# Attention and MLP on one core: the first MLP layer of the last two token chunks as seven products of quarters

## The chip, the cores and the metric

The kernel runs on one NeuronCore of a Trainium2 chip. The metric is the device time of one execution in microseconds (us), the median of three runs. The engines are called TensorE (PE in a profile; PEld is its weight load), VectorE (DVE), ScalarE (ACT), GpSimd (POOL) and SyncE (SP). SBUF is the on-chip working memory of 128 partitions, PSUM the memory in eight banks per partition into which TensorE writes its products.

## The reference

Attention with a threshold, and on its result a two-layer MLP with a squared ReLU, all in fp32.

```python
# q, k, v: (8 batches, 8 heads, 576 rows, 64); tau = 0.02
scores = q @ k.T / sqrt(64)
thresh = max(scores, axis=-1) - tau
scores = where(scores >= thresh, scores, -1e9)
attn   = softmax(scores)
x      = (attn @ v) as (8*576 = 4608 tokens, 8*64 = 512)

# w_in: (512, 2048), w_out: (2048, 512)
h   = x @ w_in
g   = maximum(h, 0) ** 2
out = g @ w_out                      # (4608, 512)
```

## The kernel before

The 4608 tokens are 18 chunks of 256. Attention runs in steps, and TensorE's matmuls of the MLP are put between the steps in small pieces. A chunk's pieces are queued when the attention output of its tokens is complete. With the last mix of attention weights and values, the chunks 15, 16 and 17 become complete together, and after it only the MLP of these three is left.

`fill` takes the pieces in order. What a piece leaves to other engines (`then`) is recorded after the next piece, so that TensorE's next matmuls stand ahead of it.

```python
P, TCH = 128, 256                  # tokens of a block and of a chunk
NMC, NFT, HF, HD = 4, 16, 8, 256   # d_model/128, d_ff/128, half of NFT, half of d_model
w_in_sb = const.tile([P, NMC, d_ff], FP32)
wo      = const.tile([P, 7, HF, HD], FP32)      # w_out in four quarters, and three sums of quarters
xT      = const.tile([P, NMC, 5 * TCH], FP32)   # attention output, a ring of five chunks
g       = const.tile([P, NFT, TCH], FP32)
gsum    = [const.tile([P, HF, P], FP32) for i in range(2)]
...
    def square_half(lo):
        f = slice(lo, lo + HF // 2)
        nc.gpsimd.tensor_tensor(out=gsum[0][:, f, :], in0=g[:, f, P:], in1=g[:, lo + HF:lo + HF + HF // 2, P:], op=ALU.add)
        nc.gpsimd.tensor_tensor(out=gsum[1][:, f, :], in0=gsum[0][:, f, :], in1=g[:, f, 0:P], op=ALU.subtract)

    def mlp_in(j, x):                           # first layer of chunk j, 128 of the 2048 columns
        f, at = FORDER[x], j * TCH % RING
        if x % 2 == 0:
            used["h"] = take("mm", (6, 7)) if j < PLAIN else next_bank()
        h = used["h"].rearrange("p (f n) -> p f n", f=2)
        for c in range(NMC):
            nc.tensor.matmul(h[:, x % 2, :], w_in_sb[:, c, f * P:(f + 1) * P], xT[:, c, at:at + TCH],
                             start=(c == 0), stop=(c == NMC - 1))
        ...
        if x % 2:
            def square():
                to = g[:, f - 1:f + 1, :]
                nc.scalar.activation(out=to, in_=h, func=AF.Relu)
                nc.gpsimd.tensor_tensor(out=to, in0=to, in1=to, op=ALU.mult)
                if j >= PLAIN and x % 8 == 7:
                    square_half(x // 8 * (HF // 2))
            posts.append(square)
        return posts
```

The second layer of all chunks but the first already works by seven products of quarters (in Strassen's manner, in Winograd's form): a chunk's g and w_out are each cut into four quarters, and seven products of quarters, or of sums of quarters, take the place of eight.

```python
    PRODUCTS = ("1", "5", "6", "2", "7", "4", "3")

    def product(j, x, half):
        if half == 0:
            used["p"] = next_bank()
        to = used["p"][:, 0:HD]
        p = PRODUCTS[x]
        ...
        g0, g1 = g[:, 0:HF, :], g[:, HF:, :]
        left, slot = {"1": (g0[:, :, 0:P], Q00), "5": (gsum[0], FT1), "6": (gsum[1], FT2), "2": (g1[:, :, 0:P], Q10),
                      "7": (gsum[0], FT3), "4": (g1[:, :, P:], FT4), "3": (gsum[1], Q11)}[p]
        for f in range(half * HF // 2, (half + 1) * HF // 2):
            nc.tensor.matmul(to, left[:, f, :], wo[:, slot, f, :], start=(f == 0), stop=(f == HF - 1))
        if not half:
            return []
        ...
        def then():
            add, sub, tt, u = ALU.add, ALU.subtract, nc.vector.tensor_tensor, u_sum
            if p == "1":
                nc.scalar.copy(p1s, to)
            elif p == "5":
                nc.scalar.copy(p5s, to)
                halves(lambda f: tt(out=gsum[0][:, f, :], in0=g0[:, f, 0:P], in1=g0[:, f, P:], op=sub))
            elif p == "6":
                tt(out=u, in0=to, in1=p1s, op=add)
                nc.gpsimd.tensor_tensor(out=osb[:, 0, HD:], in0=p5s, in1=u, op=add)
                halves(lambda f: tt(out=gsum[1][:, f, :], in0=g1[:, f, 0:P], in1=gsum[1][:, f, :], op=sub))
            ...
            else:                               # product 3, the last
                tt(out=osb[:, 0, HD:], in0=to, in1=osb[:, 0, HD:], op=add)
                return [lambda: store_rows(j, 0, 1)]
        return [then]

    def pieces_of(j):
        todo = [((x // 4 + 1) * NMC, mlp_in, j, x) for x in range(NFT)]
        if j < PLAIN:                           # PLAIN = 1: chunk 0 alone
            todo += [...]
        else:
            todo += [(n_pieces, product, j, x, half) for x in range(len(PRODUCTS)) for half in range(2)]
        return todo
```

Of the kernel before, what the change touches and what calls it, by code (L numbers as in the profile page):

```python
# [9 lines left out]
FP32 = mybir.dt.float32  # L10
U32 = mybir.dt.uint32
AF = mybir.ActivationFunctionType
ALU = mybir.AluOpType
# [6 lines left out]
def kernel(  # L20
# [10 lines left out]
    nc = tc.nc  # L31
    B, H, S, D = q.shape
    d_model, d_ff = moe_w_in.shape
    n_tokens = out.shape[0]
    P = 128
# [6 lines left out]
    NFT = d_ff // P  # L42
    TCH = 2 * P
    NCH = n_tokens // TCH
    HF, HD = NFT // 2, d_model // 2
# [6 lines left out]
    psum = ctx.enter_context(tc.tile_pool(name="psum", bufs=1, space=bass.MemoryType.PSUM))  # L52
# [4 lines left out]
    w_in_sb = const.tile([P, NMC, d_ff], FP32, name="w_in_sb")  # L57
# [7 lines left out]
    WP = 512  # L65
# [6 lines left out]
    wT = const.tile([P, NC9, S + REST], FP32, name="wT")  # L72
# [3 lines left out]
    at = RAW * 2 * WP  # L76
    w_slots = [const.tile([P, 2, S], FP32, name=f"w{i}") for i in range(2)]
# [6 lines left out]
    qT = const.tile([P, S], FP32, name="qT")  # L84
    kT = [const.tile([P, S], FP32, name=f"kT{i}") for i in range(2)]
    RING = 5 * TCH
    xT = const.tile([P, NMC, RING], FP32, name="xT")
    KB = S // 32
    NB = 2 * KB * 2 * 32
    turned = const.tile([P, 2 * NB], FP32, name="turned")  # L90
    assert 3 * 3 * WP <= 2 * NB
    g = const.tile([P, NFT, TCH], FP32, name="g")
    gsum = [const.tile([P, HF, P], FP32, name=f"gsum{i}") for i in range(2)]
# [8 lines left out]
    bank = {}  # L102
# [3 lines left out]
    n_pieces = n_in + NFT * d_model // WP  # L106
# [202 lines left out]
    used = {"tx": 0, "mm": 0, "bank": 7}  # L309

    def take(what, among):
        used[what] += 1
        return bank[among[used[what] % len(among)]]

    def next_bank():

        among = (4, 5, 6, 7) if state["step"] > first_dma + 2 else (6, 7)
        used["bank"] = min([x for x in among if x > used["bank"]] or among)
        return bank[used["bank"]]
# [144 lines left out]

    def square_half(lo):

        f = slice(lo, lo + HF // 2)
        nc.gpsimd.tensor_tensor(out=gsum[0][:, f, :], in0=g[:, f, P:], in1=g[:, lo + HF:lo + HF + HF // 2, P:], op=ALU.add)  # L470
        nc.gpsimd.tensor_tensor(out=gsum[1][:, f, :], in0=gsum[0][:, f, :], in1=g[:, f, 0:P], op=ALU.subtract)

    def mlp_in(j, x):
# [8 lines that stand above are left out]
        if x == NFT - 1:  # L482
            read_to["x"] = (j + 1) * TCH
        posts = []
        if j == PLAIN:
            posts.append(lambda: some_sums(1))
        if x % 2:
# [8 lines that stand above are left out]
# [4 lines left out]
    def some_sums(count):  # L500


        done = 16 - len(sums)
        count = min(count, (16 if state["free"] else 6 if state["rounded"] == n_pieces else 0) - done)
        for to, a, b, part in sums[:count]:
            f = slice(part * 2, part * 2 + 2)
            nc.vector.tensor_tensor(out=wo[:, to, f, :], in0=wo[:, a, f, :], in1=wo[:, b, f, :], op=ALU.subtract)  # L507
        del sums[:count]
# [21 lines left out]
    def store_rows(j, t0, t1):  # L530
        lo = j * TCH
        nc.gpsimd.dma_start(out=out[lo + t0 * P:lo + t1 * P, :].rearrange("(t p) d -> p t d", p=P), in_=osb[:, t0:t1, :])
# [5 lines left out]
    def product(j, x, half):  # L538

        if half == 0:  # L540
            used["p"] = next_bank()
        to = used["p"][:, 0:HD]
        p = PRODUCTS[x]
        if sums:
            need = {"5": 4, "6": 8, "4": 12, "7": 16}.get(p, 0)
            some_sums(max(need - 16 + len(sums), 1))
            assert state["free"]
        g0, g1 = g[:, 0:HF, :], g[:, HF:, :]
        left, slot = {"1": (g0[:, :, 0:P], Q00), "5": (gsum[0], FT1), "6": (gsum[1], FT2), "2": (g1[:, :, 0:P], Q10),
                      "7": (gsum[0], FT3), "4": (g1[:, :, P:], FT4), "3": (gsum[1], Q11)}[p]  # L550
        for f in range(half * HF // 2, (half + 1) * HF // 2):
            nc.tensor.matmul(to, left[:, f, :], wo[:, slot, f, :], start=(f == 0), stop=(f == HF - 1))  # L552
        if not half:
            return []

        def halves(fn):
            for lo in (0, HF // 2):
                fn(slice(lo, lo + HF // 2))
# [12 lines that stand above are left out]
            elif p == "2":  # L571
                tt(out=osb[:, 0, 0:HD], in0=to, in1=p1s, op=add)
            elif p == "7":
                tt(out=u, in0=to, in1=u, op=add)
                nc.gpsimd.tensor_tensor(out=osb[:, 1, HD:], in0=p5s, in1=u, op=add)
            elif p == "4":
                tt(out=osb[:, 1, 0:HD], in0=u, in1=to, op=sub)
                return [lambda: store_rows(j, 1, 2)]
            else:
                tt(out=osb[:, 0, HD:], in0=to, in1=osb[:, 0, HD:], op=add)  # L580
                return [lambda: store_rows(j, 0, 1)]
        return [then]


# [5 lines left out]
    def paired(n):  # L590

        return n >= 3 * HP
# [6 lines left out]
    PLAIN = 1  # L599

    def by_dma(n):

        return n >= 3 * HP - 1
# [6 lines left out]
    for s, (n, i) in enumerate(steps):  # L610
# [5 lines left out]
        if i in mixed:  # L616
            first, lag = mixed[i]
            cols = slice(first * P, S if by_dma(n) else min((i + 1) * P, S))
# [6 lines left out]
    chunk_at, j = {}, 0  # L625
# [12 lines left out]
    def pieces_of(j):  # L638

        todo = [((x // 4 + 1) * NMC, mlp_in, j, x) for x in range(NFT)]  # L640
        if j < PLAIN:
            todo += [(n_in + min(f + 1 + f // (NFT - 2), NFT), mlp_out, j, f) for f in range(NFT)]
        else:
            todo += [(n_pieces, product, j, x, half) for x in range(len(PRODUCTS)) for half in range(2)]
        return todo

    def add_chunk(j):
        waiting.extend(pieces_of(j))
# [17 lines left out]
    def after():  # L666
        now = state["last"]
        state["last"] = []
        for fn in state["then"]:
            state["last"] += fn() or []  # L670
        state["then"] = []
        for fn in now:
            fn()

    def fill(us):
        state["left"] += us
        while waiting and state["left"] >= PIECE_US / 2 and waiting[0][0] <= state["usable"]:
            _, fn, *what = waiting.popleft()
            state["left"] -= PIECE_US
            if fn is mlp_out or what[0] <= PLAIN and what[1] == 0:  # L680
                after()
            then = fn(*what)
            after()
            state["then"] = then
        state["left"] = min(state["left"], PIECE_US)
# [3 lines left out]
    for s, (n, i) in enumerate(steps):  # L689
        if s < HP * FIRST:  # L690
            x = int(n > 0 and i == 0)
        else:
            x = 2 if (n, i) in ((2 * HP - 2, FIRST + 1), (2 * HP - 1, FIRST + 1), (2 * HP, FIRST)) else 1
# [14 lines left out]
    for s, (n, i) in enumerate(steps):  # L708
# [20 lines left out]
        if more:  # L729
            a, b, c, d = (s + 1, s + 5, s + 7, s + 8) if paired(n) else (s + 1, s + 2, s + 4, s + 4)  # L730
# [26 lines left out]
    for s in range(END + 1):  # L757
# [9 lines left out]
        if on:  # L767
            n, i = steps[s]
            at = visits[n][1].index(i)
# [30 lines left out]
        if s in mixes and not old:  # L800
            mix(*mixes[s])
            for j in chunk_at.get(s, ()):
                add_chunk(j)
        quarter = rate(s) / 4 if s < END else 1e9
        fill(quarter)
        if s in mixes and old:
            mix(*mixes[s])
# [22 lines left out]
        if 0 < s <= NST and by_dma(steps[s - 1][0]):  # L830
            m, x = steps[s - 1]
# [54 lines left out]
```

## Time and profile before

| | |
|---|---|
| time, median of three runs | 1389.84 us (1388.68 to 1390.21) |
| span of the profiled execution | 1389.8 us, 22678 instructions |
| TensorE busy | 1354.5 us (97%) |
| VectorE, ScalarE, GpSimd busy | 828.9 (60%), 439.8 (32%), 899.3 (65%) us |
| first layers (L480) in all | 2304 matmul records, 520.4 us busy |
| second layers by seven products (L552) in all | 1904 matmul records (1088 and 816), 248.9 and 188.3 us busy |
| granted TensorE clock, mean | 0.995 of full speed |

"L480" is line 480 of the kernel; a group's row gives engine and operation, output and inputs by name, partitions by elements, the count, busy time and mean length of one, and then the idle time of the engine just before them with what ended it. Busy time is an average over stages with different limits: here the last stage, after the end of attention, is the one that the change touches, and it has to be read by itself. One product of the code (`nc.tensor.matmul`, fp32) stands in the trace as two matmul records.

### The profile page before, as it was taken

How to read it: one execution, taken by the hardware profiler on the slowest of the kernel's cores; microseconds unless marked ns; L12 is line 12 of the kernel's file. 1: busy time of each engine (PE TensorE's matmuls, PEld its weight loads, DVE VectorE, ACT ScalarE, POOL GpSimd, SP SyncE). 2: the span in 40 equal slices, each digit the busy share in tenths (PEclk: the TensorE clock that was granted, in tenths of full speed). 3: DMA queues.
4: the chain of work that ended last, by engine and by line, in shares of the span. 5: the costliest groups of instructions: out<-in, count | busy, mean ns of one | idle time of the engine just before them, and what ended most of it. 6: DMA issues, size and time to landing. Idle time of an engine off the chain costs nothing.

```text
span 1389.8 us, 22678 instructions
## 1 busy us (share of the span) xinstructions
PE 1354.5 (97%) x7576; PEld 1039.6 (75%) x7576; DVE 828.9 (60%) x1866; ACT 439.8 (32%) x1068; POOL 899.3 (65%) x1211
## 2 busy tenths in 40 slices
PE   6898999999999999999999999999999999999998
PEld 5676556777777777787777778777777877788887
DVE  5877675967767676757565757566666665401001
ACT  4776674223232323232223232322222222210110
POOL 3678875668786968686767677676867655422332
PEclk8999999999999999999999999999999999999999
DMA  8763531445545455554445355544445544310000
GB/s 154 157 152 107 143 93 29 88 85 106 115 98 115 97 109 114 105 112 94 92 87 113 76 111 107 112 87 97 93 93 91 118 89 102 64 31 16 0 16 16
DMA packets 407748, 127.95 MB, mean 92 GB/s; under 512 B 390832, under 2 KB 396752, under 8 KB 407632
## 3 DMA queue, kind: packets, MB, share of 16 engines
q1 hardware_dynamic: 385344, 94.57, 36.1%
q0 software_dynamic: 19984, 31.63, 8.4%
q8 instruction: 61, 1.00, 0.3%
q10 hardware_dynamic: 2304, 0.29, 0.2%
q14 instruction: 55, 0.45, 0.1%
HBM read 50.59 MB, written 9.44 MB: 43 GB/s over the span
## 4 chain that ended last, share of the span: by engine, by line
PE 89%; DVE 3%; ACT 3%; POOL 2%; issue 1%; DMA 1%; SPq 0%; DVEq 0%; ACTq 0%; POOLq 0%
PE bank L480 34%; PE bank L552 29%; PE s L246 12%; PE bank L432 11%; PE bank L519 2%; PE bank L330 2%; ACT wT L331 1%; ACT w L284 1%; DVE wo L507 1%; DVE w L296 1%; DVE st L268 1%; POOL g L491 0%; POOL w L306 0%; POOL w_in_sb L147 0%; DVE wo L296 0%
## 5 line engine op out<-in xcount | busy, mean ns | idle before, releaser
L480 PE MATMUL bank<-xT,w_in_sb 128*128 128x256 f32 x2304 | 520.4, 382 | 3.2 <-POOL w_in_sb L147 2.1
L480 PEld LDWEIGHTS bank<-xT,w_in_sb 128*128 128x128 f32 x2304 | 430.8, 190 | 85.8 <-issue 22.2
L268 DVE TENSOR_REDUCE st<-s 128x1 f32<-128x576 f32 x286 | 204.1, 753 | 224.4 <-PE s L246 224.3
L296 DVE SCALAR_TENSOR_TENSOR w<-s,st,w 128x576 f32<-128x576 f32 x269 | 209.2, 815 | 120.6 <-ACT w L284 120.5
L552 PE MATMUL bank<-wo,gsum 128*128 128x256 f32 x1088 | 248.9, 382 | 2.4 <-POOL gsum L470 2.4
L306 POOL TENSOR_SCALAR w<-w,st 128x576 f32<-128x576 f32 x269 | 223.5, 840 | 25.2 <-DVE st L299 19.2
L552 PEld LDWEIGHTS bank<-wo,gsum 128*128 128x128 f32 x1088 | 203.9, 190 | 41.5 <-issue 9.8
L491 POOL TENSOR_TENSOR g<-g 128x512 f32<-128x512 f32 x144 | 152.1, 1057 | 96.4 <-ACT g L490 95.1
L281 ACT ACTIVATE st<-st 128x2 f32<-128x2 f32 (+1 forms) x148 | 30.3, 205 | 566.1 <-DVE st L268 565.4
L552 PE MATMUL bank<-wo,g 128*128 128x256 f32 x816 | 188.3, 382 | 0.0
L284 ACT ACTIVATE w<-s,st 128x576 f32<-128x576 f32 x269 | 183.3, 732 | 0.2 <-ACT st L282 0.2
L370 DVE STREAM_TRANSPOSE turned<-w 128x512 f32<-128x512 f32 (+2 forms) x388 | 168.8, 490 | 18.7 <-DMA wT<-turned 16.7
L246 PE MATMUL s<-kT,qT 64*128 64x288 f32 x1016 | 166.9, 435 | 12.1 <-DVE kT L226 4.9
L304 POOL TENSOR_SCALAR st<-st 128x2 f32<-128x2 f32 (+1 forms) x148 | 32.9, 222 | 221.6 <-DVE w L296 214.4
L552 PEld LDWEIGHTS bank<-wo,g 128*128 128x128 f32 x816 | 153.0, 190 | 30.0 <-issue 8.7
L432 PE MATMUL bank<-wT,vs 128*64 128x128 f32 (+7 forms) x1700 | 167.8, 356 | 5.1 <-ACT wT L331 3.5
L432 PEld LDWEIGHTS bank<-wT,vs 128*64 128x64 f32 (+1 forms) x1700 | 95.5, 136 | 76.8 <-issue 24.6
L490 ACT ACTIVATE g<-bank 128x512 f32<-128x512 f32 x144 | 86.1, 599 | 194.8 <-PE bank L480 194.2
L246 PEld LDWEIGHTS s<-kT,qT 64*128 64x128 f32 x1016 | 94.9, 189 | 69.1 <-issue 49.0
L190 POOL DMA_DIRECT2D vs<-in_v_dram x144 | 90.7, 635 | 0.0
L566 DVE TENSOR_TENSOR gsum<-g 128x512 f32<-128x512 f32 x34 | 23.0, 707 | 110.6 <-PE bank L552 110.6
L145 POOL TENSOR_TENSOR turned<-turned 128x512 f32<-128x512 f32 x32 | 41.1, 1288 | 40.7 <-DVE turned L143 34.9
(80 smaller groups left out, 1006.1 us busy)
## 6 DMA issues: line engine op xcount, KB each, us to landing
wT<-turned SPq DMA_DIRECT2D x800, 72.0 KB, 2.3
out_dram<-osb POOLq DMA_DIRECT2D x34, 256.0 KB, 2.8
wo<-in_moe_w_in_dram SPq DMA_DIRECT2D x16, 512.0 KB, 4.7
wo<-in_moe_w_out_dram SPq DMA_DIRECT2D x16, 512.0 KB, 3.6
ql<-in_q_dram POOLq DMA_DIRECT2D x96, 72.0 KB, 2.7
wT<-turned SPq DMA_DIRECT2D x192, 36.0 KB, 2.3
kl<-in_k_dram POOLq DMA_DIRECT2D x88, 72.0 KB, 3.0
vs<-in_v_dram POOLq DMA_DIRECT2D x48, 128.0 KB, 3.1
```

The costliest lines, as they stand in the source:

```text
L190: (nc.gpsimd if state["step"] > first_dma + 2 else nc.sync).dma_start(out=to, in_=src)
L246: nc.tensor.matmul(sc[u][to, half, 0:HALF], lhsT, keys[rows, half * HALF:(half + 1) * HALF], start=True, stop=True)
L268: nc.vector.tensor_reduce(out=mx[:, u:u + 1], in_=sc[u][:, :, 0:HALF], axis=AX.XY, op=ALU.max)
L284: nc.scalar.activation(out=w[:, u, :].rearrange("p (h k) -> p h k", h=2), in_=sc[u][:, :, 0:HALF], func=AF.Exp, bias=bias[:, u:u + 1], sca ...
L296: nc.vector.scalar_tensor_tensor(out=wu, in0=sc[u][:, :, 0:HALF], scalar=thr[:, u:u + 1], in1=wu, op0=ALU.is_ge, op1=ALU.mult, accum_out=s ...
L306: nc.gpsimd.tensor_scalar(out=w[:, u, :], in0=w[:, u, :], scalar1=z[:, u:u + 1], scalar2=rcp[:, u:u + 1], op0=ALU.add, op1=ALU.mult)
L370: nc.vector.transpose(wb[:, at:at + k1 - k0, i % 2, :], w[:, u, k0 * 32:k1 * 32].rearrange("p (k q) -> p k q", q=32))
L432: nc.tensor.matmul(ps[u * D:(u + 1) * D, :], vs[n % 2][rows, u * (NBLK + 1) + c, :], wT[rows, NBLK if c == NBLK else u * (NBLK + 1) + c, a ...
L480: nc.tensor.matmul(h[:, x % 2, :], w_in_sb[:, c, f * P:(f + 1) * P], xT[:, c, at:at + TCH], start=(c == 0), stop=(c == NMC - 1))
L490: nc.scalar.activation(out=to, in_=h, func=AF.Relu)
L491: nc.gpsimd.tensor_tensor(out=to, in0=to, in1=to, op=ALU.mult)
L552: nc.tensor.matmul(to, left[:, f, :], wo[:, slot, f, :], start=(f == 0), stop=(f == HF - 1))
```

## The change

The first layer of chunks 16 and 17 is no longer computed chunk by chunk. The two chunks are taken as one matrix product: x as two halves in the 512 model columns by two chunks, w_in as two halves in its rows by two in its 2048 columns. Seven products of quarters, or of sums of quarters, take the place of eight. The point is to have less for TensorE to multiply in the stage in which nothing else is left to do.

- Twenty sums of quarters are made beforehand on VectorE (`quarter_sums`), twelve of them during the first layer of chunk 15 and eight during its second layer. Four of them overwrite a quarter of `w_in_sb`, which no later chunk needs.
- The sums lie in buffers that attention no longer needs: `wT`, the slots `w_slots`, two free places of the ring `xT`; the temporaries in `qT`, `kT` and `wT`. The second g (`g_pair`) lies in `turned`, its sums (`gsum_pair`) in `w_slots`.
- `pair_in` computes 128 columns of both halves of d_ff for both chunks in one round: 14 matmuls into four PSUM banks, two products to a bank, six banks in turn. ScalarE copies the first product, VectorE makes the four results out of the seven products and squares them.
- The second layers of 16 and 17 follow as before, the one of 17 from `g_pair` and `gsum_pair`.

```diff
-    def square_half(lo):
+    def square_half(lo, g=g, gsum=gsum):
@@ mlp_in
+        if j == PAIR - 1 and x > 1:
+            posts.append(lambda: pair_sums(1, PAIR_EARLY))
@@ product
+        g, gsum = (g_pair, gsum_pair) if j == PAIR + 1 else squares
 ...
+        if j == PAIR - 1:
+            pair_sums(1, 0)
         if not half:
             return []
@@
+    squares = g, gsum
+    PAIR = NCH - 2
+    at0, at1, at2 = (x * TCH % RING for x in (PAIR, PAIR + 1, PAIR + 2))
 ...
+    def quarter_sums():
+        add, sub = ALU.add, ALU.subtract
+        cols = [(c, slice(h * WP, (h + 1) * WP), slice(DH + h * WP, DH + (h + 1) * WP)) for c in range(2) for h in range(2)]
+        for c, lo, hi in cols:
+            yield mS1[:, c, lo], w_in_sb[:, c, hi], w_in_sb[:, 2 + c, hi], add
+        for c, lo, hi in cols:
+            yield mS2[:, c, lo], mS1[:, c, lo], w_in_sb[:, c, lo], sub
+        yield xS[0], x12, x11, sub
+        yield xS[1], x22, xS[0], sub
+        yield xS[2], x22, x12, sub
+        yield xS[3], xS[1], x21, sub
+        for c, lo, hi in cols:
+            yield w_in_sb[:, c, hi], w_in_sb[:, c, lo], w_in_sb[:, c, hi], sub
+        for c, lo, hi in cols:
+            yield xT[:, 2 * c + lo.start // WP, at2:at2 + WP], w_in_sb[:, 2 + c, lo], mS2[:, c, lo], sub
+
+    quarters = list(quarter_sums())
+    PAIR_EARLY = 8
+
+    def pair_sums(count, keep):
+        for to, a, b, op in quarters[:max(min(count, len(quarters) - keep), 0)]:
+            nc.vector.tensor_tensor(out=to, in0=a, in1=b, op=op)
+            quarters.pop(0)
+
+    def pair_in(j, f):
 ...
+        part = {1: ([w_in_sb[:, c, lo] for c in range(2)], x11), 2: ([w_in_sb[:, 2 + c, lo] for c in range(2)], x21),
+                3: (S4, x22), 4: ([w_in_sb[:, 2 + c, hi] for c in range(2)], xS[3]),
+                5: ([mS1[:, c, lo] for c in range(2)], xS[0]), 6: ([mS2[:, c, lo] for c in range(2)], xS[1]),
+                7: ([w_in_sb[:, c, hi] for c in range(2)], xS[2])}
+        if f == 0:
+            used["pair"] = [psum.tile([P, 2, 512], FP32, tag=f"s{u}", name=f"pair{u}")[:, 0, :] for u in range(2)]
+            used["pair"] += [bank[x] for x in range(4, 8)]
+        ps = {}
+        for x, what in enumerate(((1, 6), (2, 7), (5, 3), (4,))):
+            b = used["pair"][(4 * f + x) % 6].rearrange("p (h n) -> p h n", h=2)
+            for y, p in enumerate(what):
+                ps[p] = b[:, y, :]
+                for c in range(2):
+                    nc.tensor.matmul(ps[p], part[p][0][c], part[p][1][:, c, :], start=(c == 0), stop=(c == 1))
+
+        def then():
+            add, sub, tt = ALU.add, ALU.subtract, nc.vector.tensor_tensor
+            p1 = pair_p1[f % 2]
+            nc.scalar.copy(p1, ps[1])
+            u2, u3, u4, c11, c12, c21, c22 = pair_tmp[0:7]
+            tt(out=u2, in0=ps[6], in1=p1, op=add)
+            tt(out=c11, in0=ps[2], in1=p1, op=add)
+            tt(out=u3, in0=ps[7], in1=u2, op=add)
+            tt(out=u4, in0=ps[5], in1=u2, op=add)
+            tt(out=c22, in0=ps[5], in1=u3, op=add)
+            tt(out=c12, in0=ps[3], in1=u4, op=add)
+            tt(out=c21, in0=u3, in1=ps[4], op=sub)
+            for to, c in ((g[:, f, :], c11), (g[:, HF + f, :], c21), (g_pair[:, f, :], c12), (g_pair[:, HF + f, :], c22)):
+                nc.vector.scalar_tensor_tensor(out=to, in0=c, scalar=0.0, in1=c, op0=ALU.max, op1=ALU.mult)
+            if f % 4 == 3:
+                square_half(f - 3)
+            if f == HF - 1:
+                for x in (0, HF // 2):
+                    square_half(x, g_pair, gsum_pair)
+        return [then]
@@ pieces_of
+        if j >= PAIR:
+            todo = [(n_pieces, pair_in, j, f) for f in range(HF)] if j == PAIR else []
@@ fill
-            if fn is mlp_out or what[0] <= PLAIN and what[1] == 0:
+            if fn in (mlp_out, pair_in) or what[0] in (*range(PLAIN + 1), PAIR) and what[1] == 0:
                 after()
```

Rounds 0 to 7 of `pair_in` all belong to chunk 16 in the queue; chunk 17 has only its second layer left there.

More of the change, by code (lines that the diff above doesn't have):

```diff
@@ L581, in then @@
                 return [lambda: store_rows(j, 0, 1)]
+        return [then]
+    squares = g, gsum
+    PAIR = NCH - 2
+    at0, at1, at2 = (x * TCH % RING for x in (PAIR, PAIR + 1, PAIR + 2))
+    assert (at1, at2) == (at0 + TCH, at0 + 2 * TCH) and at2 + 2 * TCH <= RING
+    DH = d_ff // 2
+    wT_flat = wT.rearrange("p c n -> p (c n)")
+    mS1, mS2 = (wT_flat[:, x * 2 * DH:(x + 1) * 2 * DH].rearrange("p (c n) -> p c n", c=2) for x in range(2))
+    g_pair = turned[:, 0:NFT * TCH].rearrange("p (f n) -> p f n", f=NFT)
@@ new lines @@
+    flat_slots = [x.rearrange("p u k -> p (u k)") for x in w_slots[0:2]]
+    gsum_pair = [x[:, 0:HF * P].rearrange("p (f n) -> p f n", f=HF) for x in flat_slots]
+    xS = [flat_slots[x // 2][:, x % 2 * 2 * TCH:(x % 2 + 1) * 2 * TCH].rearrange("p (c n) -> p c n", c=2)
+          for x in range(4)]
+    x11, x12, x21, x22 = (xT[:, c:c + 2, at:at + TCH] for c in (0, 2) for at in (at0, at1))
+    temps = [x[:, 0:2 * TCH] for x in (qT, kT[0], kT[1])] + [wT_flat[:, 4 * DH:4 * DH + 6 * TCH]]
+    temps = [x[:, i:i + TCH] for x in temps for i in range(0, x.shape[1], TCH)]
@@ new lines @@
+    pair_p1, pair_tmp = temps[0:2], temps[2:]
+    def quarter_sums():
[13 more added lines that the diff above has]
+            yield xT[:, 2 * c + lo.start // WP, at2:at2 + WP], w_in_sb[:, 2 + c, lo], mS2[:, c, lo], sub
@@ new lines @@
+    quarters = list(quarter_sums())
[5 more added lines that the diff above has]
+    def pair_in(j, f):
+        assert not quarters
+        lo, hi = slice(f * P, (f + 1) * P), slice(DH + f * P, DH + (f + 1) * P)
+        S4 = [xT[:, 2 * c + f // 4, at2 + f % 4 * P:at2 + f % 4 * P + P] for c in range(2)]
+        part = {1: ([w_in_sb[:, c, lo] for c in range(2)], x11), 2: ([w_in_sb[:, 2 + c, lo] for c in range(2)], x21),
[31 more added lines that the diff above has]
+                    square_half(x, g_pair, gsum_pair)
```

## The prediction

> **What bounds the kernel now.** I read the page's busy shares first, then the chain that ended last over the closing stretch, because the change touches only the last three chunks. TensorE is busy for 97% of the span, so an end of attention or of transfers is not what sets the time. The chain from 1220 us on (start, length, what; TensorE groups by line) shows the end of the kernel to be one unbroken run of matmuls:
>
> ```profile
> 1223.88 4.72 PE bank L432 x38
> 1228.60 27.82 PE bank L480 x128
> 1256.43 24.17 PE bank L552 x112
> 1280.60 27.63 PE bank L480 x128
> 1308.23 24.17 PE bank L552 x112
> 1332.40 27.63 PE bank L480 x128
> 1360.03 24.19 PE bank L552 x112
> 1384.21 0.02 issue
> 1384.24 0.44 DVE osb L580
> 1384.67 0.29 issue
> 1384.96 0.54 POOL out_dram L532
> ```
>
> Three chunks (15, 16, 17) stand there, each a first layer (L480) and a second layer (L552), and no other engine appears until 1384.2. All three became ready with the last mix (L432) at 1228. Asked for waits of TensorE between 1228 and 1391, the trace lists none. So whatever matmul goes out of this stretch shortens the kernel by its full pace, as long as no wait comes in.
>
> The pace: one product of the code is two matmul records, so a chunk's 16 x 4 products are the 128 records of L480. 27.63 us / 128 = 0.2159 us a record, 0.4317 us a product. L552 agrees: 24.17 / 112 = 0.2158. (The mean of one record, 0.38 us, is its length in a pipeline and not the pace.)
>
> What the other engines have to spare, by stage, from the busy time in three windows: first layer of chunk 16, its second layer, first layer of chunk 17 (columns: PE, PEld, DVE, ACT, POOL busy us with counts, TensorE clock, DMA share, GB/s).
>
> ```profile
> 1280.22:1307.85 27.63, 27.63 (x130) 24.32 (x129) 0.42 (x1) 4.18 (x7) 10.32 (x10) 1.00 0.03 10
> 1307.85:1332.02 24.17, 24.17 (x113) 21.28 (x112) 4.82 (x8) 1.34 (x3) 5.94 (x6) 1.00 0.03 12
> 1332.02:1359.65 27.63, 27.63 (x130) 24.32 (x129) 0.42 (x1) 4.18 (x7) 10.32 (x10) 1.00 0.03 10
> ```
>
> VectorE is all but idle in a first layer and has 19 us free in a second one. Last, the groups of this stretch give me durations:
>
> ```profile
> L471 POOL TENSOR_TENSOR gsum<-gsum,g 128x512 f32<-128x512 f32 x6 | 7.6, 1272 | 0.5
> L470 POOL TENSOR_TENSOR gsum<-g 128x512 f32<-128x512 f32 x6 | 7.6, 1264 | 0.5
> L570 DVE TENSOR_TENSOR gsum<-g,gsum 128x512 f32<-128x512 f32 x6 | 5.4, 948 | 0.0
> L566 DVE TENSOR_TENSOR gsum<-g 128x512 f32<-128x512 f32 x6 | 4.2, 694 | 105.4 <-PE bank L552 105.4
> L568 DVE TENSOR_TENSOR u_sum<-bank,p1s 128x256 f32<-128x256 f32 x3 | 1.3, 425 | 8.2 <-PE bank L552 8.2
> L563 ACT COPY p1s<-bank 128x256 f32<-128x256 f32 x3 | 1.1, 373 | 8.7 <-PE bank L552 8.7
> ```
>
> An add of 512 columns costs VectorE 0.69 us, one of 256 columns with a PSUM operand 0.425, a ScalarE copy out of PSUM 0.373.
>
> [...]
>
> [...] L570, which runs beside GpSimd's L569, takes 948 ns where L566, of the same shape, takes 694.
>
> [...]
>
> **The change part by part.**
> (a) Removed: two first layers of 64 products each, 128 products.
> (b) Added: eight rounds (f = 0 to 7) of seven quarter products, each two products deep: 8 x 7 x 2 = 112. Same shapes (128x128 weights, 256 columns), so the same pace. Balance on TensorE: 16 products x 0.4317 = 6.91 us less. Two first layers take 55.26 us before and 48.35 after.
> (c) Second layers: unchanged in number. Chunk 17's read another g and another pair of sums.
> (d) Twenty sums of quarters on VectorE, each 512 columns: 20 x 0.69 = 13.9 us, or 19 at 0.95 where GpSimd interferes. Twelve are recorded during chunk 15's first layer, where VectorE has 27 us free: 12 x 0.95 = 11.4. Eight are recorded during its second layer, which uses 4.8 of 24.2: 8 x 0.95 = 7.6. They are ordered with the first four of seven products, so they end some 10 us before round 0. Off the path.
> (e) In each round ScalarE copies P1 and VectorE does seven adds and four squarings: 11 x 0.425 = 4.7 us, against 14 x 0.4317 = 6.04 us of TensorE. GpSimd loses the 16 squarings of L491 and gains four sums for chunk 17.
>
> The margin of (e) decides, so I lay out one round from its start at 0. The four banks of a round are full at 1.73, 3.45, 5.18 and 6.04. A reader starts about 0.25 after (before: ScalarE's L563 at 1363.56, TensorE on the next product from 1363.32). ScalarE's copy runs 1.98 to 2.35, u2 2.4 to 2.85; c11 and u3 3.7 to 4.55; u4, c22, c12 5.43 to 6.7; c21 to 7.1; the four squarings to 8.8. The next round's u2 could start at 6.04 + 2.4 = 8.45, so it starts 0.35 late and ends at 9.25, before that round's c11 can begin (9.75). The delay is absorbed in each round. TensorE comes back to a bank six bank-uses later, one and a half rounds: the bank freed by u2 at 2.85 is wanted at 9.5, the one freed by c21 at 7.1 at 13.8. No wait.
>
> (f) The way out. Call the end of round 7 T. Its c11 is squared first, by about T + 1.5; chunk 16's product 1 reads g of f = 7 only as its eighth matmul, at T + 3.0. The sum gsum[0] of the last four f can start on GpSimd when c21 is squared, T + 1.95, and ends at T + 3.3; product 5 needs that half at T + 3.45 + 1.73 = T + 5.2. gsum[1] ends at T + 4.6, wanted at T + 8.6. GpSimd's four sums for chunk 17 end near T + 9.7, wanted 24 us after T.
> (g) The output buffer osb: chunk 16's last store now comes one second layer before chunk 17 instead of two layers. Its issue follows product 3 by about 1.3 us and lands 2.8 us later (the page's median for these stores), near 4.5 us; the first new write of that row block comes after product 6, at 10.4. No wait.
> (h) The tail after the last matmul (1384.2 to 1389.8) stays.
>
> Sum: 1389.84 - 6.91 = 1382.93. I add nothing for waits and give 1382.9 us, 0.5% less.
>
> **The rivals.**
> 1. VectorE becomes the bound of the rounds. For it: 4.7 us of work in 6.04, in a strict chain, with GpSimd's sums beside rounds 4 and 5. To bind, the mean of its operations would have to exceed 6.04 / 11 = 0.55 us; the 948 ns of L570 against 694 is a factor 1.37, which makes 0.58 for those with two SBUF inputs (five of eleven), while GpSimd runs, some 2.5 us. Even squarings of 0.8 us would give 7 x 0.425 + 4 x 0.8 = 6.2, a loss of 0.15 x 8 = 1.2 us: about 1384.
> 2. A wait on the way into or out of the rounds: the quarter sums late, or f = 7's squares and sums late for products 1 and 5. Each would cost its lateness once, 1 to 3 us: 1384 to 1386. Against it: margins of 10, 1.5 and 1.9 us.
> 3. TensorE's pace falls, because weights and columns now alternate among four buffers and most bank changes carry a wait. If each of the 56 quarter products paid 0.1 us, 5.6 us would go and nearly nothing would be left, 1388.5. Against it: L480 and L552 hold the same pace with operands in different buffers, and waits long satisfied cost nothing there either (L480 changes its bank every eight products).
> 4. The schedule before 1228 moves. Against it: in the built program the order of TensorE's instructions is the same up to the end of chunk 15's second layer.
>
> **Range and chances.** The three runs before spread over 1.5 us, so a median is good to about 0.7. Below 1382.9 I see nothing to be won but that noise; above it lie rivals 1 and 2 with perhaps one chance in five. The range is 1381.7 to 1385.4. Two per cent would be 27.8 us, four times what is removed, and slower by as much would need a wait of 35 us: faster 0.01, same 0.98, slower 0.01.
>
> **What would show it.** In the profile after: the new matmul line with 224 records in a run of about 48.4 us and no TensorE idle time; VectorE's lines of a round at 0.42 us each and its busy time some 38 us in that stretch; the chain still TensorE alone until the last store. The prediction is wrong if the 224 records take over 49 us (rivals 1 and 3), if a gap stands before the first new matmul or inside products 1 and 5 (rival 2), or if the last mix no longer ends near 1228 us (rival 4).

## The result, and the profile after

The changed kernel takes 1383.32 us (1382.11 to 1384.74, 4 runs) against 1389.94 (4 runs): a ratio of 0.9955, 95% interval 0.9937 to 0.9972. Run again five times it takes 1382.53 (0.9948, 0.9936 to 0.9961, with 41 runs of before at 1390.05). The nine runs together have a median of 1383.07, 7.0 us below before. The prediction was 1382.9 and 6.91 us.

The chain that ended last, after, over the stretch shown of before in the prediction (start, length, what):

```profile
1226.83 27.82 PE bank L480 x128
1254.65 24.17 PE bank L555 x112
1278.83 3.45 PE pair L653 x16
1282.28 6.04 PE bank L653 x28
...
1327.17 42.77 PE bank L555 x199
```

Between the second layer of chunk 15 and those of 16 and 17 stand the eight rounds (L653; the name changes with the bank), and nothing but TensorE is in it. They take 1327.17 - 1278.83 = 48.34 us, where the two first layers took 27.63 + 27.63 = 55.26: 6.92 us less. From 1225 us on the trace again lists no wait of TensorE. Busy time by stage, after: the eight rounds, and the two second layers that follow (columns as before):

```profile
1278.83:1327.17 48.34, 48.34 (x225) 42.55 (x225) 30.97 (x84) 2.98 (x8) 3.19 (x3) 1.00 0.02 6
1327.17:1375.50 48.33, 48.33 (x225) 42.21 (x223) 13.06 (x23) 1.49 (x4) 13.79 (x13) 1.00 0.05 17
```

VectorE went from 0.42 us of work in a first layer to 30.97 in the eight rounds, GpSimd from 10.32 in each of two to 3.19, and TensorE did not notice.

The span of this one profile is 8.9 us shorter than before's, 1380.9 against 1389.8. That is more than 6.92, because the last mix had begun 1.8 us earlier (1222.1 against 1223.8), before anything of the change was reached. The experiments come back to it. (A span leaves out about 2 us of a timed run. The execution of before that was traced took 1391.53 us, one of the longer ones, so that its span equals the median of before only by chance.)

### The profile page after: what moved, and what is told of

Its sections match the earlier page's. It is cut to its first block, busy times and chain, and to the rows that moved or that the text cites. A ratio compares the mean times of both kernels' runs of the same rounds, so it can differ in the third digit from the quotient of the medians.

```text
span 1380.9 us, 22711 instructions
## 1 busy us (share of the span) xinstructions
PE 1345.7 (97%) x7544; PEld 1032.2 (75%) x7544; DVE 874.8 (63%) x1974; ACT 433.2 (31%) x1060; POOL 884.3 (64%) x1195
## 4 chain that ended last, share of the span: by engine, by line
PE 89%; DVE 3%; ACT 3%; POOL 2%; issue 1%; DMA 1%; POOLq 0%; SPq 0%; DVEq 0%; ACTq 0%
PE bank L480 31%; PE bank L555 29%; PE s L246 12%; PE bank L432 11%; PE bank L653 2%; PE bank L521 2%; PE bank L330 2%; PE pair L653 1%; ACT wT L331 1%; ACT w L284 1%; DVE st L268 1%; DVE wo L509 1%; DVE w L296 1%; POOL g L493 0%; POOL w L306 0%
## 5 line engine op out<-in xcount | busy, mean ns | idle before, releaser
L480 PE MATMUL bank<-xT,w_in_sb 128*128 128x256 f32 x2048 | 464.8, 383 | 3.2 <-POOL w_in_sb L147 2.1
L480 PEld LDWEIGHTS bank<-xT,w_in_sb 128*128 128x128 f32 x2048 | 382.1, 190 | 79.2 <-issue 21.7
L555 PE MATMUL bank<-wo,gsum 128*128 128x256 f32 x1024 | 234.6, 382 | 2.4 <-POOL gsum L470 2.4
L555 PEld LDWEIGHTS bank<-wo,gsum 128*128 128x128 f32 x1024 | 191.8, 190 | 39.9 <-issue 9.8
L246 PE MATMUL s<-kT,qT 64*128 64x288 f32 x1016 | 165.7, 433 | 12.3 <-DVE kT L226 5.2
L555 PE MATMUL bank<-wo,g 128*128 128x256 f32 x768 | 177.5, 382 | 0.0
L493 POOL TENSOR_TENSOR g<-g 128x512 f32<-128x512 f32 x128 | 135.9, 1063 | 62.2 <-ACT g L492 60.8
L555 PEld LDWEIGHTS bank<-wo,g 128*128 128x128 f32 x768 | 143.8, 190 | 28.7 <-issue 8.7
L492 ACT ACTIVATE g<-bank 128x512 f32<-128x512 f32 x128 | 76.6, 600 | 114.3 <-PE bank L480 113.7
L470 POOL TENSOR_TENSOR gsum<-g 128x512 f32<-128x512 f32 x32 | 41.4, 1295 | 48.0 <-DVE g L668 45.7
```

Of the source, the lines that this page charges most:

```text
L246: nc.tensor.matmul(sc[u][to, half, 0:HALF], lhsT, keys[rows, half * HALF:(half + 1) * HALF], start=True, stop=True)
```

## The experiments

The theory: the gain is the pace of the removed products and nothing else, since TensorE alone sets the end. The rivals: a part comes from the relief of GpSimd and ScalarE or from an earlier schedule; VectorE is near its limit in the rounds; the sums of quarters are hidden only just.

| kernel | median us (runs) | ratio to before, 95% interval |
|---|---|---|
| changed, again | 1382.53 (5) | 0.9948 (0.9936 to 0.9961) |
| with an eighth product | 1390.05 (12) | 1.0003 (0.9994 to 1.0011) |
| five more VectorE adds a round | 1383.13 (4) | 0.9949 (0.9934 to 0.9964) |
| ten more VectorE adds a round | 1389.85 (12) | 0.9999 (0.9991 to 1.0007) |
| all sums at the head of round 0 | 1391.36 (20) | 1.0010 (1.0003 to 1.0017) |
| all sums in one second layer | 1383.34 (4) | 0.9951 (0.9938 to 0.9965) |
| last store cut, from SyncE | 1380.73 (5) | 0.9935 (0.9923 to 0.9948) |
| and the other row block from SyncE | 1380.54 (5) | 0.9936 (0.9924 to 0.9949) |
| last store cut, and a longer warm-up | 1380.42 (5) | 0.9931 (0.9918 to 0.9945) |

**Are the removed products the whole gain?** One more product in each round, whose result nobody reads, puts 16 products back on TensorE and leaves the rest of the change in place.

```diff
+        part[8] = part[4]
-        for x, what in enumerate(((1, 6), (2, 7), (5, 3), (4,))):
+        for x, what in enumerate(((1, 6), (2, 7), (5, 3), (4, 8))):
```

> An eighth product in each round (product 4 once more, into the free half of its bank, never read): 16 products come back on TensorE, and all the rest of the change stays. Theory: the whole gain goes, +6.9 us against the changed kernel, 1390.2 us, the level of before. Rival (part of the gain comes from the lighter GpSimd and ScalarE or from an earlier start): it stays clearly below before, at 1384 to 1387 us.

1390.05 us: the kernel before, to within 0.1%. Its chain, from the first round to the second layers of 16 and 17 (the matmul line is L654 here):

```profile
1277.82 3.45 PE pair L654 x16
...
1333.08 42.77 PE bank L555 x199
```

The two stand 55.26 us apart, which is the time of two first layers before. So neither the 16 squarings that left GpSimd nor any other part of the change has a worth in time of its own that shows here; the interval leaves room for 0.8 us at most.

**How near is VectorE to its limit?** Extra adds after the squarings of rounds 0 to 6.

```diff
+            if f < HF - 1:
+                for x in range(5):          # 10 in the other kernel
+                    tt(out=pair_tmp[7 + x % 3], in0=c11, in1=c12, op=add)
```

> Five more adds of 256 columns on VectorE in each of rounds 0 to 6. At the pace of 0.34 us a round takes VectorE 16 x 0.34 = 5.4 us, below TensorE's 6.04: no change, 1383.3 us. At the length of 0.42 us a round takes 6.8, the lag grows by 0.75 a round to over 5 us and some 2 us of it come out behind the slack of product 1: 1385.5 us.

> Ten more adds of 256 columns on VectorE in each of rounds 0 to 6, nobody waits for their results. If VectorE's price for one operation is its start-to-start pace of 0.34 us, as the trace of the changed kernel shows in its runs of adds, a round takes VectorE 21 x 0.34 = 7.1 us against TensorE's 6.04, the lag grows from 3 us to about 9 by round 7, and after the slack of the banks and of product 1 some 5.8 us are left: 1389 us. If the price is the length of 0.42 us, as the prediction had it, a round takes 8.9 us and some 16 us are left: 1399 us. If VectorE had no margin at all: 7 x 10 x 0.34 = 24 us, 1407.

Five more change nothing (1383.13). Ten more cost all of the gain (1389.85, some 6.8 us above the changed kernel). This is VectorE in the second round of the run with ten, in order of time (start, length, what):

```profile
1291.70 0.42 DVE L660 TENSOR_TENSOR kT<-bank,qT 128x256 f32<-128x256 f32 x1
1292.04 0.41 DVE L661 TENSOR_TENSOR kT<-bank,qT 128x256 f32<-128x256 f32 x1
1292.37 0.41 DVE L662 TENSOR_TENSOR kT<-bank,kT 128x256 f32<-128x256 f32 x1
...
1294.69 0.75 DVE L668 SCALAR_TENSOR_TENSOR turned<-wT 128x256 f32<-128x256 f32 x2
1295.36 3.44 DVE L671 TENSOR_TENSOR wT<-kT,wT 128x256 f32<-128x256 f32 x10
1298.71 0.42 DVE L660 TENSOR_TENSOR kT<-bank,qT 128x256 f32<-128x256 f32 x1
```

Each operation is 0.41 to 0.42 us long, yet the next begins 0.33 to 0.34 after it. (None of these reads what the one just before it wrote; u3, L662, reads u2 of two before.) From u2 to u2 the round takes 1298.71 - 1291.70 = 7.01 us for 21 operations. All of TensorE's waits in this run from 1225 us on (what waited, for what, total us, times, longest):

```profile
PE bank L555 <- DVE g L668: 3.5, 1, 3.5
PE pair L653 <- DVE kT L660: 0.7, 1, 0.7
PE bank L653 <- DVE kT L660: 0.2, 1, 0.2
```

The lag comes out where it was expected, mostly at product 1's eighth matmul, which needs g of f = 7. The waits sum to 4.4 us of idle time; counted from the start of one record to the start of the next, these places cost 5.0. The other 1.8 us are the pace after the longest wait: the 34 records from 1336.68 to 1345.81 take 9.13 us and not 7.34, and in the 4 us from 1337 on TensorE's granted clock is 0.59. The expectation of 5.8 us had left this out.

**What is hiding the sums worth?** All twenty at the head of round 0; and, the other way, all twenty recorded within the second layer of chunk 15, two to each half product.

```diff
 # at the head of round 0
-            posts.append(lambda: pair_sums(1, PAIR_EARLY))
+            pass
-            pair_sums(1, 0)
+            pass
-        assert not quarters
+        pair_sums(len(quarters), 0)
 # in the second layer alone
-    PAIR_EARLY = 8
+    PAIR_EARLY = 20
-            pair_sums(1, 0)
+            pair_sums(2, 0)
```

> All twenty sums of quarters at the head of round 0 and none earlier. Theory: twenty sums at a pace of 0.62 us are 12.4 us; product 1 needs none, product 6 needs ten of them (6.9 us after the start), product 7 fifteen, product 3 nineteen (12.4 us), where TensorE would be there at 4.3: 8 us of waiting in round 0 and perhaps 1 or 2 more if TensorE's clock falls in the gaps, 1391 to 1393 us, slower than before. Rival (the sums hardly matter for the time, since TensorE has other work to bring forward): within 2 us of the changed kernel.

> All twenty sums during the second layer of chunk 15, two to each half product, none during its first layer. Theory: VectorE uses 4.8 of 24.2 us there, 20 x 0.62 = 12.4 us more fit, and its work for products 7 and 3 has some 5 us to spare: no change, 1383.3 us. Rival (the sums hold up VectorE's and GpSimd's part of the second layer): 1 to 4 us more, with a gap of TensorE before product 7 or 3 of chunk 15.

At the head the change becomes a loss, 1391.36. Its round 0 on TensorE (the wait in brackets; four records are one quarter product):

```profile
1278.88 1.03 PE L653 MATMUL pair<-xT,w_in_sb 128*128 128x256 f32 x4
1285.74 2.08 PE L653 MATMUL pair<-w,wT 128*128 128x256 f32 x4 [5.84 <-DVE w L632]
1287.61 1.92 PE L653 MATMUL pair<-xT,w_in_sb 128*128 128x256 f32 x4
1289.32 1.16 PE L653 MATMUL pair<-w,w_in_sb 128*128 128x256 f32 x4
1290.31 1.03 PE L653 MATMUL bank<-w,wT 128*128 128x256 f32 x4
```

Product 1 needs no sum and runs; product 6 waits 5.84 us for ten of them. Then a quarter product comes every 1.87 and 1.71 us in place of 0.86, until about 1289.3. TensorE's granted clock is 0.89 on the mean from 1278 to 1284 us, 0.54 from 1284 to 1290 and 1.00 from 1290 to 1320. Because TensorE was held up by its clock meanwhile, products 7 and 3 found their sums done (the trace lists no other wait), and round 0 ends some 8.0 us late in all (round 1 begins at 1292.90, 14.0 us after round 0, and not 6.04). Recorded in the second layer alone, the sums cost nothing (1383.34, no TensorE wait in the trace). But that run does not show what its expectation asked, whether VectorE has room for all twenty there. Its second layer begins at 1254.77, and this is VectorE around the first layer:

```profile
1229.87 0.69 DVE L632 TENSOR_TENSOR w<-xT,w 128x512 f32<-128x512 f32 x1
1260.22 0.69 DVE L571 TENSOR_TENSOR gsum<-g 128x512 f32<-128x512 f32 x1 [29.66 <-PE bank L555]
```

The operation at 1229.87 is the tenth sum: ten of the twenty ran from 1223.54 to 1230.56, as soon as VectorE came to them, and only the other ten within the second layer, where VectorE is then busy for 10.7 of 24.2 us and done with the last at 1271.5, 7.4 us before round 0. The place in the code set their order on VectorE and not their time. (In the run with all of them at the head of round 0 they could not start early, because in VectorE's order they stand behind chunk 15's last add, at 1279.08.)

**Did the change move anything ahead of the last mix?** The changed kernel and the one before, each as it is, for second traces.

> The changed kernel once more, for a tighter ratio and a second trace. Theory (only the 16 removed products count, 6.9 us, and the 1.8 us by which the first profile was ahead at the last mix came from a faster start of that one execution): 1383 us, 0.995 of before; in the trace the stretch from the last mix to the last matmul is again 6.9 us shorter than before's, while the moment of the last mix may differ by up to 2 us. Rival (the change also moves something ahead of the last mix): the last mix always stands near 1222 us, 1.8 us earlier than before.

> The kernel before once more, for a second trace of it. Theory (the place of the last mix changes from execution to execution of the same kernel, by whether the first scores run at TensorE's full or half pace): 1389.9 us; the eight records of the first scores take either 2.3 or 1.25 us, and with 1.25 the last mix stands near 1222 us and not 1223.9. Rival: 1223.9 again whatever the first scores do.

The second trace of the changed kernel again has the stretch from the last mix (1222.16) on 6.9 us shorter; the second one of before stands at 1223.77, with first scores as in its first trace. That pair alone could not decide, since in both traces of before the first scores took 2.30 us and in both of the changed kernel 1.25. The run with ten adds decides it: a changed kernel, in whose trace the first scores take 2.30, and its last mix stands at 1223.67. The run with an eighth product is the other end, with 1.25, and 1.95 in place of 2.99 for the group of scores near 22 us; its last mix stands at 1221.04. So the place of the last mix goes with TensorE's pace in the first 30 us of an execution. The first scores and the group near 17 us of the trace before, the same of the trace after, then the first scores of the run with ten adds:

```profile
8.64 2.30 PE L246 MATMUL s<-kT,qT 64*128 64x288 f32 x8 [0.88 <-DVE ntau L753]
...
17.76 2.30 PE L246 MATMUL s<-kT,qT 64*128 64x288 f32 x8 [4.91 <-DVE kT L226]
```

```profile
8.45 1.25 PE L246 MATMUL s<-kT,qT 64*128 64x288 f32 x8 [0.68 <-DVE ntau L847]
...
16.00 2.30 PE L246 MATMUL s<-kT,qT 64*128 64x288 f32 x8 [5.24 <-DVE kT L226]
```

```profile
8.69 2.30 PE L246 MATMUL s<-kT,qT 64*128 64x288 f32 x8 [0.93 <-DVE ntau L850]
```

By the group near 17 us the trace before is already 1.76 us behind, all of the difference at the last mix. The 1.8 us were of the execution and not of the kernel. The timed runs say the same: with an eighth product the changed kernel is level with before.

**A version that beats both.** The only serial piece left behind the last matmul is its add and its store. The last store is cut by columns; the half finished early is sent early, and the last half goes from SyncE's queue.

```diff
 # product 2
+                if j == NCH - 1:
+                    return [lambda: nc.sync.dma_start(out=out[j * TCH:j * TCH + P, 0:HD], in_=osb[:, 0, 0:HD])]
 # product 3
+                if j == NCH - 1:
+                    return [lambda: nc.sync.dma_start(out=out[j * TCH:j * TCH + P, HD:], in_=osb[:, 0, HD:])]
                 return [lambda: store_rows(j, 0, 1)]
```

> A version that may beat both: the changed kernel with the last store cut in two by columns, the finished half sent after product 2 and the last half (128 KB in rows of 1 KB) from SyncE's queue in place of GpSimd's. What is left behind the last matmul (5.4 us in the first profile) is the only serial piece of the last 160 us that is not TensorE's pace. Theory: GpSimd's 0.54 us of issuing and some of the landing time go, 0.5 to 1 us less, 1382.4 us. Rival (the landing and the end of the program set the tail whatever the queue): no change that can be measured, 1383.3.

1380.73 us, about 2.3 below the nine runs of the changed kernel, where 0.5 to 1 was expected. The ends of the two traces, changed kernel first (SPq is SyncE's queue):

```profile
1375.56 0.42 DVE L585 TENSOR_TENSOR osb<-bank,osb 128x256 f32<-128x256 f32 x1 [3.03 <-PE bank L555]
1376.28 0.54 POOL L534 DMA_DIRECT2D out_dram<-osb  x1 [2.65 <-DVE osb L585]
```

```profile
1375.96 0.42 DVE L587 TENSOR_TENSOR osb<-bank,osb 128x256 f32<-128x256 f32 x1 [3.03 <-PE bank L555]
1376.42 0.37 SPq L589 DMA_DIRECT2D out_dram<-osb  x1
```

From the start of the add to the end of the issue 1.26 us have become 0.83. From there to the end of the span (1380.9 and 1379.2) 4.1 have become 2.4. The median time from the start of an issue to its landing went from 2.3 to 1.8; after the landing the span goes on for 2.3 us in the one and 1.0 in the other, so about 1.3 us of the difference lie there. Some 0.35 us more lie outside the span: the timed run of the changed kernel is 2.1 us longer than its span, that of this kernel 1.75. The size of the last transfer and its queue were changed together; which of them did how much was not separated. Two more kernels asked whether GpSimd's other store matters too, and whether a longer warm-up (24 transposes before the first scores in place of 20) removes the spread from one execution to the next.

> The version with the cut last store (1380.7 us), with the store of the other row block of chunk 17 sent from SyncE's queue too, so that GpSimd issues no transfer in the last 25 us. It asks where that version's gain of about 2 us over the changed kernel came from, more than the 0.5 to 1 us expected. Theory (only what follows the last transfer counts: with a store from GpSimd's queue as the last one the program ends 2.8 us after its data moved, with SyncE's 1.3 us after): no further change, 1380.7 us. Rival (any use of GpSimd's queue near the end lengthens the end of the program): up to 1 us less.

> The version with the cut last store, and 24 in place of 20 of the transposes that keep TensorE busy before the first scores (they end at about 8.6 us in place of 7.8, so no idle gap is left). It asks what makes the executions of one kernel fall on levels about 1.3 us apart (1388.8, 1390.1, 1391.4 for the kernel before). Theory (the level is how many of the first groups of scores run at half of TensorE's pace): fewer of them do, the upper levels grow rare and the median falls by 0.5 to 1.3 us, to 1379.5 to 1380.2. Rival (the levels do not hang on it): the same as without, 1380.7.

The other store makes no difference that can be measured (1380.54), so the gain is put down to the last store. The longer warm-up makes none either (1380.42, 1379.20 to 1380.67); in its trace the first scores took 1.25 us, as they did without it, the group near 22 us took 2.99, and 0.41 us of idle time were still left ahead of the first scores. What decides the pace of these early groups in an execution stays open: from 8.6 to 10.8 us the granted clock reads 1.00 in the trace before as in the trace after, though the one ran at about half the other's pace.

## Why the prediction was right, point by point

- **What bounds the kernel.** TensorE's unbroken run after the last mix, with no wait: right, and still so after. The eighth product shows it from the other side.
- **(a) to (c), the balance of products.** 112 for 128 at an unchanged pace, 6.91 us and 48.35 for the rounds: measured 6.92 and 48.34. The runs' medians give 7.0.
- **(d), the sums.** Off the path, as written. The last one ended at 1267.9, 10.9 us before round 0 (some 10 predicted), though they did not run in the layers where they were recorded: the first twelve were done by 1231.5, and only four started in the second layer. Their price was set too high: 0.69 us is the length of one, and four in a row take 2.53 us, 0.61 for each further one. In the run with all twenty in a row they take 12.3 us and not 13.9 to 19. Only that run felt it.
- **(e), the round.** The layout was right in its order and its waits (u2, c11 and u4 of round 0 began 2.33, 3.66 and 5.38 us after its start at 1278.66, against 2.4, 3.7 and 5.43). The price of VectorE was mis-sized, for the same reason: 11 x 0.425 = 4.7 us by lengths, where the window shows 30.97 / 8 = 3.9 of busy time (30.97 us in all, some 38 forecast) and the pace in a run of operations is 0.33. The squarings of round 0 ended 8.1 us after its start, not 8.8, and the lag of 0.35 us did not arise: in the next round u2 waited for ScalarE's copy (0.24 us) and not for VectorE. GpSimd's account was wrong too: it lost the 16 squarings but gained no sums, since chunk 17's four were there before (in the closing stretch L470 and L471 have six operations each before and after); they only moved behind round 7. As (d) and (e) lie off the path, the measured time did not test their prices; the runs with ten adds and with all sums at the head did.
- **(f), the way out.** From the start of product 1 (T, 1327.01): f = 7's c11 was squared at T + 1.1 (predicted 1.5), gsum[0] done at 2.9 (3.3), gsum[1] at 4.3 (4.6), the sums for chunk 17 at 10.3 (9.7). No wait.
- **(g), (h), the output buffer and the tail.** No wait on the stores; 5.4 us behind the last matmul against 5.6.
- **Rival 1, VectorE the bound.** Rightly set low, and further off than written: by the pace the limit is 6.04 / 0.33 = 18 operations a round against 11, and the runs with 16 (no cost) and 21 (6.8 us) stand on its two sides. Interference with GpSimd's sums did occur. The four squarings of every round, and in rounds 3 and 7 the last two, beside GpSimd, from the groups and the order of time after:

```profile
L668 DVE SCALAR_TENSOR_TENSOR turned<-wT 128x256 f32<-128x256 f32 x16 | 8.2, 553 | 0.0
L668 DVE SCALAR_TENSOR_TENSOR g<-kT 128x256 f32<-128x256 f32 x8 | 3.4, 419 | 0.0
L668 DVE SCALAR_TENSOR_TENSOR g<-wT 128x256 f32<-128x256 f32 x8 | 3.3, 418 | 0.0
```

```profile
1298.13 0.75 DVE L668 SCALAR_TENSOR_TENSOR turned<-wT 128x256 f32<-128x256 f32 x2
...
1304.18 1.83 DVE L668 SCALAR_TENSOR_TENSOR turned<-wT 128x256 f32<-128x256 f32 x2
1304.41 1.31 POOL L470 TENSOR_TENSOR gsum<-g 128x512 f32<-128x512 f32 x1 [24.27 <-DVE g L668]
```

  The 0.425 us that the prediction takes for a squaring as for an add was its author's estimate; it holds where GpSimd is idle (418 and 419 ns). Beside GpSimd's sum two of them took 1.83 us and not 0.75, a factor of 2.4 where the prediction had 1.37; and four operations of eleven have two SBUF inputs, not five. It happens in two rounds of eight, at their end, and the slack took it.
- **Rivals 2 and 3, waits at the edges and a slower pace.** Neither came: no wait, and 0.2158 us a record (48.34 / 224).
- **Rival 4, the earlier schedule.** Rightly excluded, but the sign named for it was a poor one. The last mix did end 1.8 us away from its place in the first trace, by the execution and not by the change. The stretch from the last mix on is the sign to read.

## What to carry to other kernels

Here TensorE ran without a wait to the end. The change was worth the pace of what it removed there (6.92 us for 16 products), and its new work on VectorE cost nothing up to a limit (16 operations a round were free, 21 cost 6.8 us). That limit came out right when an operation was priced by the start-to-start time in a run of them (0.33 us), and not by the length of one (0.42). Making operands ahead paid because it was hidden; the same twenty sums at the head of round 0 turned a gain of 7 us into a loss (1391.36 us against 1390.05). The place of the sums in the code set their order on VectorE and not their time (ten of those recorded in a layer that began at 1254.77 us had run by 1230.56); when work runs is read from the trace. When two profiles differ by more than the change explains, compare them from the last point that the change can't have touched.

## What the runs showed that was not expected

- VectorE's price in a row is below its length: 0.33 us against 0.42 at 256 columns, 0.61 against 0.69 at 512, with a PSUM operand at 256 as well. Where an operation reads what the one just before it wrote, the price was higher in the two cases read, both of xS[1]: it began 0.71 us after xS[0] with all sums at the head (the next, which reads neither, 0.61 after that), and 0.79 after it in the changed kernel (the next 0.61 after that).
- The executions of one kernel gather on levels. Of 41 runs of the kernel before, 9 lie at 1388.75 to 1389.07, 27 at 1389.63 to 1390.36 and 5 at 1391.32 to 1391.40 us. The levels are less sharp than that: of 40 further runs of it, five lie between, at 1389.29 to 1389.59. The traces at hand fit levels made by how many of the first groups of scores run at half of TensorE's pace (traces of before and of the run with ten adds at 1391.5 us with 2.30 for the first group, the one of the run with an eighth product at 1389.0 with 1.25 and, for the group near 22 us, 1.95). That the groups make the levels was argued from these traces and not tried: the one attempt to move them, the longer warm-up, moved nothing.
- With the last store from GpSimd's queue (256 KB) the span ended 2.3 us after the landing, from SyncE's (128 KB) 1.0 after it. What fills that time is not explained. Neither is it why a timed run is 2.1 us longer than its span in the changed kernel and about 1.75 both before and with the last store cut.
